# A Fourier layer and a gated convolution on one core: the first batch's feature D/2 through the FFT, five narrowings shared between two engines, and batch 2's folds in earlier steps

## The chip, the cores and the metric

The kernel runs on one core of a Trainium2 chip. A core has five engines that work side by side, each through its own queue in order: TensorE (PE) multiplies matrices, VectorE (DVE) and ScalarE (ACT) work element by element, GpSimd (POOL) does small element work and issues indirect loads, SyncE (SP) issues transfers. ACT and POOL issue some transfers too. Waits between engines are semaphores. The metric is device time in microseconds: the median of three runs. A profile of one further execution shows what each engine did and when.

## The reference

The input x has 8 batches of 3136 rows and 256 columns. Each batch goes through a two-dimensional Fourier transform, of which the real part is kept, and then through a gated feed-forward layer with a three-tap convolution along the rows:

```python
X = np.fft.fft(x, axis=1)
X = np.fft.fft(X, axis=2)
a = X.real.astype(np.float32)

h = np.maximum(a @ w_in, 0.0)                    # 256 -> 1024
hp = pad(h, one row of zeros on each side)
conv_out = sum(conv_w[k] * hp[:, k:k + S, :] for k in range(3))
gate = 1.0 / (1.0 + np.exp(-conv_out))
return (h * gate @ w_out).astype(np.float32)     # 1024 -> 256
```

x is float32. The weights `w_in` (256 x 1024), `conv_w` (3 x 1024) and `w_out` (1024 x 256) arrive as float64, and the kernel makes float32 of them itself: that is a narrowing.

## The kernel before

**The transform.** Rows n and S - n, and columns d and D - d, are folded onto each other, so that the transform over rows becomes a few real products with cosine and sine tables. For each batch VectorE folds the input: `fold_ops(b)` gives 14 operations, seven for each half of x, which end in two tiles `w` of folded features. TensorE multiplies these with the tables (`tabs`, in a version for even and one for odd rows) in units (`units(b)`): matrix products, then a copy by ScalarE (`copy`), then sums by VectorE (`fin`). The results are PT and QT (`PQ[b]`), with 1569 row frequencies each. The transform over columns is merged with `w_in` into a matrix `G` (`blocks(i)`, `column(i)`). The product with PT (`pa`) and the product with QT (`pb`) give by their sum a front row, and by their difference the mirrored back row.

**Feature D/2** (column 128 of x) has only a cosine part, and it does not fit into the 128 partitions of PT beside the other 128. For batches 1 to 7 the class `Feature` computes its transform as a 56 x 56 FFT: a gather of the 3136 single elements, tables made on ScalarE (`tables`), and four stages (`stage`: matrix products, two twiddle products on VectorE, matrix products, a copy and a store to `ed` in DRAM). `spread` reads `ed` back, repeated over all partitions, into `eb`. `seed(s)` writes `eb` times a column `ge` into the bank `pa` before the products of step s add to it. For batch 0 before the change, the odd half of this feature stands in row 127 of QT and the even half in a tile `ea`; a unit `feature` and a row `er` on one partition collect both. The first four steps add it by a one-row product of `er` and `left`; from the fifth step on `seed` is used, and two steps write the whole bank `pa` once beforehand (`start_all`).

**The loop.** A step s is one of 8 batches, 4 chunks of row frequencies and 8 blocks of 128 hidden features: 256 steps, 32 for each batch. A cycle t works on several steps at once, and the loop at the end of the kernel gives the order in every queue: `sigmoid` of step t - 2, `products` and `copies` of step t + 1, `combine` of step t, `seed` of step t + 2, `first_tap` of step t, `other_taps` of step t - 1, `gate` of step t - 2, `mm2` of step t - 3. The first 20 steps (`triple`) let TensorE add the sine product to `pa` once more, so that VectorE combines only the back rows.

**Work beside the steps** is put into cycles by hand with `at(cycle, where, fn)`, and `where` says at which place of a cycle it runs. The list `ends` holds for each batch the cycle in which its folds end and its units start; the folds of batch b run from `ends[b - 1]` to `ends[b]`, its units from `ends[b]` to three cycles before its first step. `free` moves a fold to a later cycle where one is `taken`. The loads of batch b + 1 follow the folds of batch b at a fixed distance.

**The start.** SyncE loads the first half of x of batch 0; GpSimd issues four indirect loads of mirrored rows, writes one element that lets SyncE load the second half (`held`), issues four more, and writes one element that lets the tables load. VectorE folds. TensorE meanwhile multiplies folded data into an unused bank (`keep_on`), so that it is busy before the first real product. The order behind it is: narrow the first quarter of `w_in`, mirror the tables on ScalarE, four odd units, narrow the second quarter, the even units, `blocks(0)`, narrow the third quarter, and the steps. The fourth quarter is narrowed in cycle 0, `w_out` in cycles 2, 3, 5 and 7.

**A narrowing** is seven VectorE operations on 512 elements of each partition: three make the exponent, one puts the sign in, two make the mantissa, and one multiplies them.

Of the kernel before, what the change touches and what calls it, by code (L numbers as in the profile page):

```python
# [30 lines left out]
FIRST = 4  # L31
# [7 lines left out]
def kernel(  # L39
# [33 lines left out]
    ep = ctx.enter_context(tc.tile_pool(name="ep", bufs=2))  # L73
    erp = ctx.enter_context(tc.tile_pool(name="erp", bufs=1))
# [28 lines left out]
    xh, wt, ea = {}, {}, {}  # L103
# [3 lines left out]
    sg = const.tile([P, 2, 2], F32, name="sg")  # L107
    nc.gpsimd.memset(sg[:, 0], -1.0)
    nc.gpsimd.memset(sg[:, 1], 1.0)
# [33 lines left out]
    def fold_ops(b):  # L143
# [3 lines left out]

        def half(h):
# [27 lines left out]
            def feats(odd):  # L176
                def f():
                    if h == 0 and odd:
                        wt[b] = [wp.tile([P, 4, HQ, P], F32, name="w", tag="w%d" % i) for i in range(2)]
                        if b == 0:  # L180
                            ea[b] = ep.tile([P, 2, HQ], F32, name="ea", tag="ea")
                            nc.gpsimd.memset(wt[b][0][0:KR, 2:4, :, P - 1:P], 0.0)
# [6 lines left out]
                    if b:  # L189
                        nc.gpsimd.memset(wt[b][odd][k, 2:4, qs, P - 1:P], 0.0)  # L190
                    elif odd:
                        gt(w[k, 2:4, qs, P - 1], t()[k, 7:5:-1, :, P], sg[k], op=ALU.mult)
                    else:
                        nc.gpsimd.tensor_copy(ea[b][k, :, qs], v[:, :, :, P])
# [10 lines left out]
    PQ, eb, er = {}, {}, {}  # L205
# [36 lines left out]
    class Unit:  # L242

        def __init__(self, b, mms, copy, fin, own=False):
            self.own, self.b, self.mms, self.copy_, self.fin_ = own, b, mms, copy, fin

        def matmuls(self, i, n):
            if i == 0:
                self.p = spare() if self.b == 0 and not self.own else psd.tile([P, 512], F32, name="pd", tag="pd")
# [22 lines left out]
    def units(b):  # L272
# [54 lines left out]
        def feature():  # L327

            mms = []
            for i in range(2):  # L330
                for j, qs in enumerate(((3, 1), (2, 0))):
                    for c in range(2):
                        n = HO // 2 + 1 - c
                        o = 32 * (2 * j + c)
                        mms.append(product((slice(o, o + 1), slice(0, n)),
                                           lambda k, q, c=c: ea[b][0:k, c, q:q + 1], 0, qs[i],
                                           slice(c, HE, 2), i == 0, i == 1))

            def copy(p):
                a_["e"] = [asp.tile([P, HO + 2], F32, name="as", tag="as") for _ in range(2)]  # L340
                for j in range(2):
                    for c in range(2):
                        n = HO // 2 + 1 - c
                        o = 32 * (2 * j + c)
                        nc.scalar.copy(out=a_["e"][c][0:1, j * n:(j + 1) * n], in_=p[o:o + 1, 0:n])

            def fin(p):
                t = er[b]
                nh = HO // 2
                for c in range(2):  # L350
                    n = nh + 1 - c
                    a, bb = a_["e"][c][0:1, 0:n], a_["e"][c][0:1, n:2 * n]
                    gt(t[:, 2 * c:Q4 + 1:4], a, bb, op=ALU.add)
                    gt(t[:, M - 2 * c:Q4:-4], a[:, 0:nh], bb[:, 0:nh], op=ALU.subtract)
            return Unit(b, mms, copy, fin, True)

# [3 lines left out]
        def row():  # L360
            er[b] = erp.tile([1, NK], F32, name="er", tag="er")
            nc.sync.dma_start(out=er[b], in_=PQ[b][1][P - 1:P, :])
# [257 lines left out]
    def start_all(p, l, r):  # L620

        mm(p, l, r, True, True)
# [333 lines left out]
```

## Time and profile before

| what | us |
|---|---|
| runs | 1223.03, 1222.69, 1222.80 |
| median | 1222.8 |
| the profiled execution, and its span | 1223.94, 1222.2 |
| first element operation of the folds | 8.38 |
| tables in place, mirroring starts | 22.95 |
| first product of the first unit | 25.77 |
| first product of step 0 | 44.3 |
| first product of step 1 (cycle 0 starts) | 47.4 |
| start of cycle 36 | 234.8 |
| start of cycle 125 | 642.8 |

The span runs from the first to the last instruction of the program in the profile; the profiled execution's own time lies 1.7 us above it. The profile names engines PE, DVE, ACT, POOL and SP as above, and PEld for the loading of weights into TensorE. A row of the timeline has a start, a duration, engine, line of the kernel, operation and tiles, out<-in; the brackets give idle time of the engine before it, and what ended that. All matrix products stand under line 94, so they are told apart by their tiles: `pb` and `pa` are the products of a step, `po` the output products of a step (and, at the start, spare banks), `pd` the products of the units and of the FFT.

### The profile page before, as it was taken

Reading aid. Unit: us, or ns where it says so; the run is one execution under the profiler, and the core shown is the slowest. Engines: PE = TensorE matmul, PEld = TensorE weight load, DVE = VectorE, ACT = ScalarE, POOL = GpSimd, SP = SyncE. Lnnn points to the kernel's source line nnn. Section 1 sums busy time; section 2 is a strip of 40 time slices with the busy share of each in tenths; the row PEclk is TensorE's granted clock in tenths of the full one; section 3 lists DMA queues with packets and bytes.
Section 4 is the critical chain, followed back from the end, with each engine's and each line's share of the span. In section 5 each row is a group of like instructions: output and inputs, shape, how many; then the busy total and the mean of one; then the engine's idle time right before and its main releaser. Section 6 shows DMA issues by size and latency. Waiting matters only on the chain.

```text
span 1222.2 us, 15450 instructions
## 1 busy us (share of the span) xinstructions
PE 1187.9 (97%) x4876; PEld 907.5 (74%) x4876; DVE 1126.0 (92%) x1696; ACT 877.0 (72%) x1832; POOL 370.9 (30%) x474
## 2 busy tenths in 40 slices
PE   5999999999999999999999999999999999999998
PEld 4676777667777777677777777777777787777776
DVE  7799978998999999999999999999998888899996
ACT  2467666777677777777777777777777777788884
POOL 5224532244142413242324242232222122222222
PEclk9999999999999999999999999999999999999999
DMA  9512242112031210211111020310001000110000
GB/s 235 180 8 79 81 48 60 54 54 72 6 99 42 75 50 32 76 55 53 53 57 59 22 79 27 86 47 26 27 1 53 31 26 27 46 33 27 26 27 31
DMA packets 70213, 66.30 MB, mean 54 GB/s; under 512 B 28123, under 2 KB 57827, under 8 KB 70131
## 3 DMA queue, kind: packets, MB, share of 16 engines
q1 hardware_dynamic: 64493, 52.18, 15.0%
q0 software_dynamic: 5120, 12.85, 3.4%
q8 instruction: 39, 0.64, 0.2%
q14 instruction: 43, 0.35, 0.1%
q10 hardware_dynamic: 518, 0.28, 0.1%
HBM read 39.53 MB, written 25.74 MB: 53 GB/s over the span
## 4 chain that ended last, share of the span: by engine, by line
PE 68%; DVE 22%; issue 4%; ACT 2%; DMA 0%; DVEq 0%; SPq 0%; ACTq 0%
PE po L94 42%; PE pb L94 10%; PE pa L94 10%; DVE g L698 7%; PE pd L94 7%; DVE h L686 4%; DVE g L719 3%; DVE xh L158 2%; DVE xh L169 1%; ACT nb L675 1%; DVE w L186 1%; DVE w L187 1%; DVE xh L173 0%; ACT g L711 0%; DVE pt L291 0%
## 5 line engine op out<-in xcount | busy, mean ns | idle before, releaser
L94 PE MATMUL po<-wout,g 128*128 128x256 f32 x3072 | 709.9, 381 | 13.8 <-DVE g L719 13.3
L94 PEld LDWEIGHTS po<-wout,g 128*128 128x128 f32 x3072 | 579.0, 190 | 168.8 <-DVE g L719 50.7
L698 DVE SCALAR_TENSOR_TENSOR g<-h,cw,g 128x770 f32<-128x770 f32 (+1 forms) x512 | 548.9, 1072 | 9.3 <-ACT g L692 0.2
L718 POOL TENSOR_TENSOR g<-g,h 128x385 f32<-128x385 f32 (+1 forms) x256 | 232.5, 909 | 781.3 <-ACT g L711 523.1
L711 ACT ACTIVATE g<-g 128x385 f32<-128x385 f32 (+2 forms) x512 | 244.4, 527 | 196.8 <-DVE g L698 196.2
L675 ACT ACTIVATE nb<-pb 128x386 f32<-128x386 f32 (+2 forms) x472 | 208.1, 494 | 85.9 <-PE pb L94 85.2
L686 DVE CUSTOM_DVE_ANT_0 h<-pa,nb 128x386 f32<-128x386 f32 (+2 forms) x492 | 255.6, 559 | 3.7 <-ACT h L672 3.7
L692 ACT ACTIVATE g<-h,cw 128x770 f32<-128x770 f32 (+1 forms) x256 | 243.4, 951 | 0.2 <-DVE h L686 0.2
L94 PE MATMUL pb<-qt,G 127*128 127x387 f32 (+2 forms) x512 | 212.8, 496 | 0.0
L94 PE MATMUL pa<-pt,G 128*128 128x387 f32 (+2 forms) x512 | 211.9, 495 | 0.0
L641 ACT ACTIVATE pa<-eb,ge 128x387 f32<-128x387 f32 (+2 forms) x252 | 151.7, 602 | 1.3 <-PE pa L94 0.7
L94 PEld LDWEIGHTS pa<-pt,G 128*128 128x128 f32 x512 | 96.9, 189 | 73.5 <-issue 17.9
L719 DVE TENSOR_TENSOR g<-g,h 128x385 f32<-128x385 f32 (+1 forms) x256 | 146.2, 571 | 0.9 <-ACT g L711 0.9
L94 PE MATMUL pd<-tab,w 98*128 98x196 f32 (+3 forms) x448 | 122.5, 374 | 0.0
L133 POOL DMA_INDIRECT xh<-in_x_dram,idx x64 | 106.5, 1665 | 13.4 <-issue 9.6
L94 PEld LDWEIGHTS pb<-qt,G 127*128 127x128 f32 x512 | 94.6, 190 | 17.4 <-issue 0.9
L94 PEld LDWEIGHTS pd<-tab,w 98*128 98x128 f32 (+1 forms) x448 | 84.0, 191 | 12.5
L738 ACT COPY os<-po 128x256 f32<-128x256 f32 x196 | 57.6, 394 | 8.4 <-PE po L94 4.6
L158 DVE TENSOR_TENSOR xh<-xh 98x1020 f32<-98x1020 f32 (+1 forms) x32 | 40.8, 1283 | 2.4 <-DMA xh<-in_x_dram,idx 2.4
L169 DVE TENSOR_TENSOR xh<-xh 98x1024 f32<-98x1024 f32 (+1 forms) x32 | 42.1, 1314 | 0.1
L291 DVE TENSOR_TENSOR qt<-as,pd 128x197 f32<-128x197 f32 (+1 forms) x14 | 7.2, 516 | 21.7 <-ACT as L287 21.7
L291 DVE TENSOR_TENSOR pt<-as,pd 128x197 f32<-128x197 f32 (+1 forms) x14 | 7.3, 520 | 20.2 <-ACT as L287 20.2
(114 smaller groups left out, 405.6 us busy)
## 6 DMA issues: line engine op xcount, KB each, us to landing
out_dram<-os SPq DMA_DIRECT2D x192, 128.0 KB
xh<-in_x_dram SPq DMA_DIRECT2D x16, 784.0 KB
eb<-ed SPq DMA_DIRECT2D x16, 193.5 KB
tab<-dft_seq_dram SPq DMA_DIRECT2D x4, 589.5 KB
raw<-in_moe_w_in_dram SPq DMA_DIRECT2D x4, 512.0 KB
raw<-in_moe_w_out_dram SPq DMA_DIRECT2D x1, 2048.0 KB
eb<-ed SPq DMA_DIRECT2D x8, 209.0 KB
eb<-ed SPq DMA_DIRECT2D x8, 193.0 KB
```

The source lines that it names most:

```text
L94: nc.tensor.matmul(o, l, r, start=start, stop=stop, skip_group_check=True)
L133: nc.gpsimd.indirect_dma_start(out=xh[b, h][0:NP, 7 - m].rearrange("p q d -> p (q d)"), out_offset=None, in_=bass.AP(tensor=x.tensor, offs ...
L158: vt(a[:, :, :, 1:D], a[:, :, :, 1:D], r[:, :, :, D - 1:0:-1], op=ALU.add)
L641: act(pa[s][:, 0:n], eb[b, c], AF.Copy, scale=ge[:, f:f + 1])
L675: act(nb[s][:, i, cols], p[:, cols], AF.Copy, scale=-1.0 if i else 1.0)
L686: nc.vector._custom_dve(TENSOR_ADD_SAT, out=to, in0=a[:, cols], in1=c[:, i, cols], s0=BIG, s1=0.0)
L692: act(gs[s], hs[s][:, 0:n], AF.Copy, scale=cw[:, 0, s[2]:s[2] + 1])
L698: stt(out=g, in0=h[:, k:k + n], scalar=cw[:, k, f:f + 1], in1=g, op0=ALU.mult, op1=ALU.add)
L711: act(gs[s][:, c], gs[s][:, c], AF.Sigmoid)
L718: gt(g[:, p], g[:, p], h[:, p], op=ALU.mult)
L719: vt(g[:, v], g[:, v], h[:, v], op=ALU.mult)
L738: nc.scalar.copy(out=osb[:, j % 2], in_=pt[:, j % 2])
```

## The change

The change does three things, with what follows from them.

Batch 0's feature D/2 goes through the same FFT as the other batches'. The gather is issued by ScalarE right behind the load of the convolution weights, then come the table rows (`load`, which was a part of `place`). ScalarE makes the FFT's tables before it mirrors the others; the four stages stand between the sixth and the seventh of the first half's folds; GpSimd issues the first `spread`. The row `er`, the unit `feature`, the one-row products, the copies to `left` and `start_all` go. Every step gets a seed, so `column(0)` comes before `blocks(0)` and `column(1)` before the loop. Eight filler products of 512 columns take the place of sixteen of 256; two of them write both banks of `pa`.

In five narrowings (the fourth quarter of `w_in` and all of `w_out`) ScalarE makes the exponent by one Relu in place of two VectorE operations, `left` serves as room for the mantissa, and the sign comes in later.

The folds of batch 2 run in cycles 20 to 35, those of batch 3 from 36 to 60, those of batch 4 from 61 to 92; the units of batches 2, 3 and 4 start at 36, 61 and 93. The last operations of batch 1's units no longer keep folds out of their cycles.

```diff
     def feats(odd):
...
-        if b:
-            nc.gpsimd.memset(wt[b][odd][k, 2:4, qs, P - 1:P], 0.0)
-        elif odd:
-            gt(w[k, 2:4, qs, P - 1], t()[k, 7:5:-1, :, P], sg[k], op=ALU.mult)
-        else:
-            nc.gpsimd.tensor_copy(ea[b][k, :, qs], v[:, :, :, P])
+        nc.gpsimd.memset(w[k, 2:4, qs, P - 1:P], 0.0)
...
+        def load(self):
+            n = (RC + NQ - 1) // NQ
+            for r, v in enumerate(self.l):
+                for s in range(2):
                     w = v.shape[2]
                     nc.scalar.dma_start(out=v[1:1 + n * NQ, s], in_=bass.AP(
...
-        def gather(self, b, b0):
-            nc.sync.dma_start(out=self.y[self.K, b - b0].unsqueeze(2), in_=bass.AP(
+        def gather(self, b, b0, eng):
+            eng.dma_start(out=self.y[self.K, b - b0].unsqueeze(2), in_=bass.AP(
...
-    def narrow(dst, raw):
+    low = const.tile([P, 1], F32, name="low")
+    nc.gpsimd.memset(low, -896.0 * 2 ** 23)
+    def narrow(dst, raw, room):
...
         ts(out=d, in0=hi, scalar1=20, scalar2=0x7FF, op0=lsr, op1=ALU.bitwise_and)
-        ts(out=d, in0=d, scalar1=-896, scalar2=0, op0=ALU.add, op1=ALU.max)
-        ts(out=d, in0=d, scalar1=23, scalar2=None, op0=lsl)
-        stt(out=d, in0=hi, scalar=-0x80000000, in1=d, op0=ALU.bitwise_and, op1=ALU.bitwise_or)
-        ts(out=hi, in0=hi, scalar1=0xFFFFF, scalar2=0x100000, op0=ALU.bitwise_and, op1=ALU.bitwise_or)
-        stt(out=lof, in0=lo.bitcast(U32), scalar=2.0 ** -32, in1=hi, op0=ALU.mult, op1=ALU.add)
+        if room is not None:
+            act(d, d, AF.Relu, scale=2.0 ** 23, bias=low[0:d.shape[0]])
+        else:
+            ts(out=d, in0=d, scalar1=-896, scalar2=0, op0=ALU.add, op1=ALU.max)
+            ts(out=d, in0=d, scalar1=23, scalar2=None, op0=lsl)
+            stt(out=d, in0=hi, scalar=-0x80000000, in1=d, op0=ALU.bitwise_and, op1=ALU.bitwise_or)
+        sg = hi
+        if room is not None:
+            c, n = hi.shape[1:]
+            sg = room[:, 0:c * n].rearrange("p (c n) -> p c n", c=c)
+        ts(out=sg, in0=hi, scalar1=0xFFFFF, scalar2=0x100000, op0=ALU.bitwise_and, op1=ALU.bitwise_or)
+        stt(out=lof, in0=lo.bitcast(U32), scalar=2.0 ** -32, in1=sg, op0=ALU.mult, op1=ALU.add)
+        if room is not None:
+            stt(out=d, in0=hi, scalar=-0x80000000, in1=d, op0=ALU.bitwise_and, op1=ALU.bitwise_or)
         stt(out=dst, in0=lof, scalar=2.0 ** -20, in1=dst, op0=ALU.mult, op1=ALU.mult)
...
+    feat = Feature()
     w_cv.load(nc.scalar)
+    feat.place()
+    feat.gather(0, 0, nc.scalar)
+    feat.load()
     for h in range(2):
         for f in load_ops(0, h, nc.sync, nc.scalar, h == 1):
             f()
...
         act(pa[s][:, 0:n], eb[b, c], AF.Copy, scale=ge[:, f:f + 1])
...
-        mm(pa[s][:, 0:n], G[:, 0, fs], PQ[b][0][:, ch.k0:ch.k1], first(s), not triple(s))
-        if first(s):
-            mm(pa[s][:, 0:n], left[0:1, f, :], er[b][:, ch.k0:ch.k1], False, False)
+        mm(pa[s][:, 0:n], G[:, 0, fs], PQ[b][0][:, ch.k0:ch.k1], False, not triple(s))
...
-    def keep_on(n):
-        for _ in range(n):
-            mm(idle[:, 0:2 * P], wt[0][1][0:NP, 1, 0], wt[0][1][0:NP, 0, 0:2], True, True)
+    def keep_on(banks):
+        for p in banks:
+            mm(p.rearrange("p (s q d) -> p s q d", s=2, q=2), wt[0][1][0:NP, 1, 0], wt[0][1][0:NP, 0:2, 0:2],
+               True, True)
...
-    nc.gpsimd.memset(PQ[0][1][96:P, :], 0.0)
-    for f in fold_ops(0):
+    for i in range(3):
+        feat.tables(i)
...
+    ops = fold_ops(0)
+    for f in ops[0:6]:
         f()
+    for i in range(4):
+        feat.stage(i, 0, 1)
+    for f in ops[6:]:
+        f()
+    spread(0, [0], nc.gpsimd)
...
-    keep_on(16)
+    keep_on([idle] * 6)
+    keep_on([psa.tile([P, 512], F32, name="pa", tag="pa") for _ in range(2)])
...
-    flip()
-    store()
-    spread(0, range(len(chunks)))
+    spread(0, range(1, len(chunks)))
     for f in load_ops(1, 0, nc.sync):
         f()
+    column(0)
     blocks(0)
...
-    at(0, "dve", lambda: w_in[3].narrow(0, 2))
-    for i in (0, 1):
-        at(i, "pe", lambda i=i: column(i))
+    room = left.rearrange("p f i -> p (f i)").bitcast(I32)
+    at(0, "dve", lambda: w_in[3].narrow(0, 2, room))
     for cycle, c in ((2, 0), (3, 2), (5, 4), (7, 6)):
-        at(cycle, "dve", lambda c=c: w_out.narrow(c, c + 2))
+        at(cycle, "dve", lambda c=c: w_out.narrow(c, c + 2, room))
...
-    ends = [9] + [max(26 * b - 6, per * (b - 1) - 3) for b in range(1, B)]
+    ends = [9, 20, per + 4] + [per * (b - 1) - 3 for b in range(3, B)]
...
-            taken.add(cs[i + 1])
+            if b > 1:
+                taken.add(cs[i + 1])
...
     copies(steps[0])
+    column(1)
```

## The prediction

> **What bounds the kernel now.** I read the page first, then busy times by stretch, then waits and timeline at the start and around one narrowing.
>
> ```profile
> PE 1187.9 (97%) x4876; PEld 907.5 (74%) x4876; DVE 1126.0 (92%) x1696; ACT 877.0 (72%) x1832; POOL 370.9 (30%) x474
> PE 68%; DVE 22%; issue 4%; ACT 2%; DMA 0%; DVEq 0%; SPq 0%; ACTq 0%
> ```
>
> Both PE and DVE are nearly full, and the chain of what ended last changes between them: the answer differs by stretch. A cycle t of the loop starts with the pb product of step t+1. From those starts I cut the run: cycles 0-8 are 47.4 to 97.1, 9-19 to 151.8, 20-35 to 234.8, 36-60 to 352.2, 61-92 to 497.9, 93-124 to 642.8, 125-156 to 785.7. Columns: stretch, length, then busy us of PE, PEld, DVE, ACT, POOL, clock, DMA share, GB/s.
>
> ```profile
> 0.00:44.30 44.30, 28.62 (x127) 22.21 (x127) 33.94 (x62) 12.38 (x27) 22.09 (x38) 1.00 0.83 235
> 47.40:97.10 49.70, 48.24 (x198) 33.47 (x197) 44.82 (x67) 30.33 (x61) 8.59 (x18) 1.00 0.30 56
> 97.10:151.80 54.70, 52.76 (x211) 37.82 (x210) 54.28 (x68) 39.55 (x99) 29.52 (x27) 1.00 0.24 74
> 151.80:234.80 83.00, 80.79 (x338) 61.01 (x338) 72.62 (x118) 55.38 (x116) 20.04 (x29) 1.00 0.26 50
> 234.80:352.20 117.40, 114.58 (x470) 87.43 (x469) 111.06 (x168) 84.29 (x175) 41.13 (x45) 1.00 0.20 60
> 352.20:497.90 145.70, 144.06 (x590) 110.10 (x589) 138.26 (x212) 107.05 (x223) 49.02 (x61) 1.00 0.18 57
> 497.90:642.80 144.90, 142.38 (x581) 108.27 (x580) 138.10 (x212) 107.37 (x223) 46.63 (x58) 1.00 0.17 55
> 642.80:785.70 142.90, 142.61 (x591) 110.61 (x590) 134.84 (x208) 108.18 (x224) 45.31 (x56) 1.00 0.16 50
> ```
>
> PE's own work needs no busy column: near the end six 256-column matmuls (twelve passes) take 2.59 us and a whole cycle 3.89, so a column costs 1.69 ns. Summed over each stretch's matmuls that gives 46.7, 51.1, 78.7, 112.2, 141.4, 139.7 and 141.4 us for the seven stretches from 47.4 on. The lengths exceed it by 3.0, 3.7, 4.3, 5.2, 4.3, 5.2 and 1.5. The last has 32 cycles with folds and DFT spread over all of them, and nearly no loss; the four before alternate cycles in which DVE has a fold and PE nothing extra (4.6 us against 3.9) with cycles in which PE has DFT matmuls (5.2). Batch 2 is the clearest: folds in 20-45, DFT in 46-60.
>
> The start, first the waits, then the timeline:
>
> ```profile
> ACT tab L239 <- DMA tab<-dft_seq_dram: 16.0, 1, 16.0
> PE pb L94 <- POOL w L188: 8.7, 1, 8.7
> DVE xh L158 <- DMA xh<-in_x_dram,idx: 2.4, 1, 2.4
> ```
>
> ```profile
> 2.01 1.19 POOL L133 DMA_INDIRECT xh<-in_x_dram,idx  x1 [0.26 <-issue]
> 12.98 0.09 POOL L575 MEMSET tab<- 1x1 f32 x1
> 13.10 1.40 SPq L219 DMA_DIRECT2D tab<-dft_seq_dram  x2
> 15.36 5.06 PE L94 MATMUL pb<-w 98*128 98x256 f32 x11 [8.66 <-POOL w L188]
> 19.79 6.14 PE L94 MATMUL pb<-w 98*128 98x256 f32 x22
> ```
>
> POOL issues eight mirrored loads in order; its memsets behind the fourth and the eighth release SP's next loads, so POOL paces all input. PE's fillers run until 25.9, when the DFT starts.
>
> One narrowing (cycle 2):
>
> ```profile
> 57.89 0.56 DVE L686 CUSTOM_DVE_ANT_0 h<-pa,nb 128x385 f32<-128x385 f32 x1 [2.82 <-ACT h L672]
> 58.36 0.42 DVE L515 TENSOR_SCALAR wout<-raw 128x512 int32<-128x512 int32 x1
> 63.86 0.49 ACT L672 ACTIVATE h<-pa 128x385 f32<-128x385 f32 x1 [0.37 <-PE pa L94]
> ```
>
> The ACT row is step 3's relu, behind which the new exponent operation will stand; here it comes 5 us after DVE has its exponent bits.
>
> **What the Trainium skill says.** "ScalarE: Activation LUTs", What ACT_TABLE_LOAD costs: an ACTIVATE with a per-partition pointer takes about 280 ns + 0.833 ns an element; 921 for 770 elements, and the trace has 938: agrees. "TensorE: Matmul & The Clock Gate", What's actually happening: full clock only after a busy window of about 3.4 us that is not aligned to the kernel. The eleven slow filler passes (0.46 us, then 0.28) agree in kind. "DMA: Bandwidth & Descriptors", Queues, rings and completion order: an engine takes turns between its queues packet by packet; no row here shows a gather beside full loads. "GPSIMD Engine Reference", Specifications: POOL shares SBUF interfaces with DVE. Agrees: the two-tap operation takes 1.51 us at 63.31 beside POOL's gate, usually 1.04.
>
> **The change part by part.**
>
> *Front.* POOL gets two iotas, a sign operation that waits for DVE, and four memsets before its first load: 0.2 + 0.16 + 0.19 + 0.90 (their rows at 78-84 us) + about 0.25 of handing over = 1.7 us, and with it the held half of x and the tables. DVE's second fold needs the fourth load (landed 9.39, issue now ends 8.75): I put 1.5 on DVE. The two twiddle products, 112 elements, by the 336-element row (488 ns) less 224 elements[...], are 0.25 each: DVE +2.0 behind them. The gather (three in 64.6-71.1, 0.63 to 0.78 of the DMA engines: 1.75 us of all of them each) and the table rows (0.76) must fit before 10 us, where the share leaves 2.4 us idle; I take 0 beyond the 1.7. Fillers now stand behind the second FFT stage: evens end 15.9 + 1.5, products 0.5, matmuls about 0.9: start 18.8 instead of 15.36. The columns are equal (16 x 256, 8 x 512). At the old 10.5 us they end 29.3, at full clock (6.9) 25.7, when the tables (22.9 + 1.7, then 1.97 of mirroring) bind at 26.6. Bounds for the start of the DFT: +0.8 to +3.6; I take +2.5. Twenty table operations on ACT (4.7 us) lie in its 16 us wait; ACT's issues (1.9 + 4 x 0.77) push the zero rows to 8.6, needed at 17.1: 0. POOL's eb load waits for the feature's store (about 22) and fits POOL's 12.1 us of idleness before 38.37; batch 1's mirrored loads behind it start at 41.6. SP loses two row transfers and one eb load: 0.
>
> *To the first combine.* Out go the feature's matmuls (0.88) and one copy row (0.86), in comes the column (0.97). But DVE's third narrowing, 43.2 to 47.3, is what combine(0) then waits for: 47.35 instead of 48.14, so -0.8.
>
> *Cycles 0-8.* PE loses four one-row products (0.65), the other copy row (0.86) and two 512-column starts (0.86 each), with what lies ahead: 46.7 to 40.3. DVE loses two operations of 0.46 in each of five narrowings: 46.7 to 42.1 by rows. DVE becomes the bound. The exponent costs ACT an estimated 706 ns (first page); DVE covers 1.2 us with the two mantissa operations. Laying the rows of each engine in queue order, DVE waits 0.9 in cycle 0, 3.0 in cycle 2 (step 3's products stand behind blocks, and ACT behind a table load), 0 in cycle 3, 0.5 in 5 and 7: 5.0, against 2.8 now. So 42.1 + 5.0 = 47.1 instead of 49.5: -2.4. Four added seeds (0.59) lie in ACT's idle 1.9 us before each relu; uncovered they cost 0.59 each. The work moved out of cycles 5-13 (ACT, POOL) was hidden: 0, at most -1.
>
> *Cycles 9-19*: DVE-bound by folds that stay: 0.
>
> *Cycles 20-124.* DFT sums stay; folds move. DVE by rows (3.40 a cycle, 3.7 in a last chunk, 1.2 a fold, 0.55 to 0.94 a finish): 20-35 rises 72.8 to 81.3 against PE's 78.7; 36-60 falls to 109.0 against 112.2; 61-92 to 134.6 (141.4); 93-124 to 134.6 (139.7). In 20-28 both have 47 to 49, in 29-35 DVE 33.9 against 29.7: 49.0 + 1.5 + 33.9 = 84.4, +1.5. The others get a loss like that of 125-156, more for 36-60, which inherits DVE's backlog: 114.0, 143.0, 142.0: -3.4, -2.7, -3.0. Together -7.6; bounds -11 and 0. The folds' companions move with them: batch 3's plain load and three zero rows pass output stores on SP, its eight mirrored loads (1.67 us each) and batch 2's feature copies pass gates on POOL. POOL is busy for a quarter to a third of these stretches, and a gate's half is needed a cycle later by PE: 0; a gate that did wait behind a mirrored load would cost PE up to 1 us, eight times. SP never waits long here: 0. Stages of the other batches' FFT stay at 14-18 and 31-35.
>
> *Rest* unchanged in order: 0.
>
> Sum: +2.5 - 0.8 - 2.4 + 0 - 7.6 = -8.3. The profiled execution took 1223.94 (span 1222.2), 1.1 above the median of 1222.8; on the median: **1214.5**.
>
> **Rivals.**
>
> R1, the exponent waits stay as the trace has them. Exponent bits are ready at 49.04, 58.78, 66.09, 76.92, 88.29; the relus ahead end at 51.09, 64.35, 69.78, 79.72, 88.94. Adding 0.7 and taking off 1.2 of cover: 1.6, 5.1, 3.2, 2.3, 0.2 = 12.4 instead of 5.0: 1222. Against: PE is lighter, so the relus come sooner.
>
> R2, spreading gains nothing, because DVE is the bound in 20-60 and its sum (459.5 us in 20-124) is the same: +7.6, 1222. Against: 125-156, where the same sums lose 1.5.
>
> R3, slower: the gather lands late. DVE, ACT and PE all stand in order behind it, before folds, mirroring and fillers. The engines are full (0.99, 1.05) from 10 to 32 us; 3,136 small packets taking turns with 2 KB ones would last until then. Products at 33 instead of 17.4 cost 15.6: 1230. It decides from a landing after 17.4 us, and the gain is gone at 26. Against: idle shares before 10 us and a held second half.
>
> R4, fewer waits in 0-8 and bound -11: 1208.
>
> **How the numbers follow.** Forecast 0.58, R1 0.14, R2 0.10, R3 0.13, R4 0.05. The forecast's own range, from the front's bounds and those of cycles 20-124, is 1209 to 1220. I give 1207 to 1225, which leaves out R3 and a thin low edge. Within 0.2% (2.4 us) is what one cannot tell from no change: most of R1, R2 and the forecast's upper edge, 0.19. Faster 0.66, slower 0.15.
>
> **What would show it.** First mirrored load at 3.7, fillers from about 19, DFT from 28, first product near 46.5; the twiddle products without a wait before them. Five DVE waits on the exponent operation, the longest in cycle 2, 5 us together; four more seeds. 36-124 at about 399 us instead of 408, 20-35 a little longer. A DVE wait for the gather, or a filler start past 22, makes it R3; waits of 12 us, R1.

## The result, and the profile after

The changed kernel took 1223.4 us (median of 4 runs, 1223.07 to 1226.01) beside 1222.8 for the kernel before on the same chip: ratio 1.0009, 95% interval 0.9992 to 1.0027. No change can be told. Forecast was 1214.5. The profiled execution took 1223.58, with a span of 1221.8.

The page of the changed kernel, busy times and the engines' shares of the chain:

```profile
PE 1180.9 (97%) x4834; PEld 902.0 (74%) x4834; DVE 1120.5 (92%) x1688; ACT 880.8 (72%) x1835; POOL 366.7 (30%) x468
PE 72%; DVE 19%; issue 4%; ACT 3%; DMA 2%; POOL 0%; DVEq 0%; SPq 0%; ACTq 0%; POOLq 0%
```

TensorE and VectorE lost 7.0 and 5.5 us of work, and the span hardly moved. In the chain, the share of DMA rises from 0 to 2%. Busy times of the changed kernel, cut at the same cycles as before (columns: stretch, length, busy us of PE, PEld, DVE, ACT, POOL, clock, DMA share, GB/s):

```profile
0.00:52.10 52.10, 29.62 (x109) 19.29 (x109) 35.28 (x66) 13.56 (x45) 19.78 (x44) 1.00 0.97 242
54.90:101.60 46.70, 41.52 (x168) 29.95 (x168) 39.46 (x56) 32.55 (x65) 6.40 (x11) 1.00 0.15 20
101.60:156.40 54.80, 52.83 (x211) 37.80 (x210) 54.38 (x68) 36.80 (x79) 29.53 (x27) 1.00 0.25 74
156.40:241.50 85.10, 82.31 (x338) 61.94 (x338) 80.72 (x129) 55.13 (x116) 29.44 (x37) 0.98 0.31 67
241.50:357.20 115.70, 114.54 (x469) 87.04 (x468) 110.17 (x166) 83.94 (x175) 39.30 (x44) 1.00 0.20 60
357.20:500.10 142.90, 142.60 (x590) 110.40 (x589) 135.01 (x208) 108.55 (x224) 46.01 (x56) 1.00 0.16 50
500.10:642.50 142.40, 141.44 (x582) 108.78 (x582) 134.65 (x209) 108.47 (x224) 45.49 (x57) 1.00 0.16 53
```

| stretch | before | after | difference | forecast |
|---|---|---|---|---|
| to the first product of step 0 | 44.3 | 52.1 | +7.8 | +2.2 |
| from there to cycle 0 | 3.1 | 2.8 | -0.3 | -0.5 |
| cycles 0-8 | 49.7 | 46.7 | -3.0 | -2.4 |
| 9-19 | 54.7 | 54.8 | +0.1 | 0 |
| 20-35 | 83.0 | 85.1 | +2.1 | +1.5 |
| 36-60 | 117.4 | 115.7 | -1.7 | -3.4 |
| 61-92 | 145.7 | 142.9 | -2.8 | -2.7 |
| 93-124 | 144.9 | 142.4 | -2.5 | -3.0 |

(The forecast's first product near 46.5 is +2.2; its +2.5 and -0.8 make +1.7 for the first two rows together.) Behind the first product the loop gained 8.1 us, and the front lost 7.8. The DMA share of the front rose from 0.83 to 0.97.

Two rows of the front before, and then the timeline of the changed front:

```profile
8.38 2.35 DVE L158 TENSOR_TENSOR xh<-xh 98x1020 f32<-98x1020 f32 x2 [2.40 <-DMA xh<-in_x_dram,idx]
22.95 1.97 ACT L239 ACTIVATE tab<-tab 99x392 f32<-99x392 f32 x4 [16.03 <-DMA tab<-dft_seq_dram]
```

```profile
13.90 1.22 DVE L151 TENSOR_TENSOR xh<-xh 98x1020 f32<-98x1020 f32 x1 [2.15 <-DMA xh<-in_x_dram,idx]
20.17 0.44 DVE L397 TENSOR_TENSOR ft<-pd,ft 56x112 f32<-56x112 f32 x2
20.67 0.95 PE L91 MATMUL pd<-ft 56*29 56x56 f32 x8 [4.63 <-DVE ft L397]
21.54 8.71 PE L91 MATMUL pb<-w 98*128 98x512 f32 x12
31.81 2.14 PE L91 MATMUL po<-tab,w 98*128 98x196 f32 x8
35.02 6.22 PE L91 MATMUL po<-tab,w 98*128 98x196 f32 x24 [1.06 <-ACT tab L224]
21.65 0.20 ACT L406 COPY ft<-pd 29x56 f32<-29x56 f32 x1 [3.24 <-PE pd L91]
32.65 0.24 ACTq L408 DMA_DIRECT2D ed<-ft  x1
33.06 1.90 ACT L224 ACTIVATE tab<-tab 99x392 f32<-99x392 f32 x4 [11.21 <-DMA ed<-ft]
```

Three things are to be read from it. VectorE's second fold waits 2.15 us for a mirrored load and starts at 13.90; before, the two stood together from 8.38. The twiddle products stand behind six folds, the second FFT product behind them, and the fillers behind that: they start at 21.54 instead of 15.36. ScalarE has the FFT's result at 21.85 and issues its store at 32.65; the mirroring, which is next in its queue, starts at 33.06 instead of 22.95, and TensorE pauses 1.06 us for it in its first DFT. What held the store is in the chain of waits of the same kernel (start, duration, what):

```profile
8.56 13.18 DMA xh<-in_x_dram
21.75 0.02 issue
21.76 10.81 DMA tab<-dft_seq_dram
32.57 0.02 issue
32.59 0.02 ACTq L408
32.65 0.43 DMA ed<-ft
33.07 1.90 ACT tab L224 x4
```

In the compiled program the transfers of SP and ScalarE take turns over eight semaphores (the records of the trace name them), and each waits until the transfer eight places ahead of it has landed. The gather and the four table rows move every later transfer by five places. So the first load of the other table waited for the second half of x (21.75), and ScalarE's store of 6 KB for that table (32.57).

The DMA engines in the first 20 us, in 40 slices of 0.5 us: share in tenths, GB/s, and the queue that carries ScalarE's transfers (packets, MB, share of 16 engines). First the kernel before:

```profile
DMA  0005349999997785957789999998998999998998
GB/s 0 0 0 70 57 160 336 356 291 291 303 303 176 213 250 172 291 98 201 270 336 369 315 287 217 262 205 197 250 211 220 297 306 226 264 277 239 340 222 202
q10 hardware_dynamic: 61, 0.04, 0.8%
```

Then the changed kernel:

```profile
DMA  0006647999999997897998899999999989999999
GB/s 0 0 0 70 35 115 213 350 348 299 191 60 7 40 177 107 189 262 194 275 208 212 248 232 262 299 229 250 222 221 203 235 197 226 239 240 220 272 218 220
q10 hardware_dynamic: 3463, 0.24, 17.9%
```

Between 5.5 and 7 us the engines are busy for 0.9 of the time or more and move 60, 7 and 40 GB/s, where they moved 303, 176 and 213: the gather's 4-byte packets have their turn. ScalarE's queue takes 17.1% of sixteen engines more, 3.4 us of all of them. About half of that went into slices before 10 us that had been idle (their mean share rises from 0.67 to 0.83). The second fold is 4.4 us late. In a later run without the small packets it is 1.7 us late, about the 1.4 by which GpSimd's first load is issued later (3.43 instead of 2.01); the other 2.7 are the small packets' part.

### The profile page after: what moved, and what is told of

Same layout as the page of the kernel before. It is cut to its first block, busy times and chain, and to the rows that moved or that the text cites. A ratio compares the mean times of both kernels' runs of the same rounds, so it can differ in the third digit from the quotient of the medians.

```text
span 1221.8 us, 15368 instructions
## 1 busy us (share of the span) xinstructions
PE 1180.9 (97%) x4834; PEld 902.0 (74%) x4834; DVE 1120.5 (92%) x1688; ACT 880.8 (72%) x1835; POOL 366.7 (30%) x468
## 3 DMA queue, kind: packets, MB, share of 16 engines
HBM read 39.54 MB, written 25.74 MB: 53 GB/s over the span
## 4 chain that ended last, share of the span: by engine, by line
PE 72%; DVE 19%; issue 4%; ACT 3%; DMA 2%; POOL 0%; DVEq 0%; SPq 0%; ACTq 0%; POOLq 0%
PE po L91 45%; PE pb L91 11%; PE pa L91 10%; DVE g L643 6%; PE pd L91 6%; DVE h L631 3%; DVE g L664 3%; DVE xh L151 2%; ACT nb L620 1%; DMA xh<-in_x_dram 1%; DMA tab<-dft_seq_dram 1%; DVE xh L162 1%; DVE w L176 1%; DVE w L177 1%; ACT g L656 0%
## 5 line engine op out<-in xcount | busy, mean ns | idle before, releaser
L91 PE MATMUL pd<-tab,w 98*128 98x196 f32 (+3 forms) x448 | 126.7, 374 | 0.0
L178 POOL COPY w<-xh 98x4 f32<-98x4 f32 (+1 forms) x32 | 20.4, 639 | 33.1 <-DVE xh L162 17.5
```

The lines of the kernel that those rows point to most:

```text
L91: nc.tensor.matmul(o, l, r, start=start, stop=stop, skip_group_check=True)
```

## The experiments

Each run is compared with the kernel before on its own chip; the first product is that of step 0 in its profile. A profile shows where the time of one execution goes, the medians what an edit is worth.

### The loop's edits without the front

```diff
 # kernel before, plus
-    ends = [9] + [max(26 * b - 6, per * (b - 1) - 3) for b in range(1, B)]
+    ends = [9, 20, per + 4] + [per * (b - 1) - 3 for b in range(3, B)]
-            taken.add(cs[i + 1])
+            if b > 1:
+                taken.add(cs[i + 1])
 # e1_old_front also: narrow(dst, raw, room), with
+    room = left[:, NF // 2:NF].rearrange("p f i -> p (f i)").bitcast(I32)
```

> The kernel before with the loop's two edits only: the new placing of folds and finishes, and the exponents of five narrowings on ScalarE (their spare tile is the other half of `left`, which is free in the first cycles). Batch 0's feature stays the old way, and so does the whole front. Theory A, the loop's gain is real and the front alone lost it: first product at 44.3 as before, cycles 9 to 124 shorter by about 5 us, cycles 0 to 8 by about 1.5 (their other gain came from the dropped one-row products): 1216.3 us, faster by 0.5%. Rival B, the loop's gain in the changed kernel only made up for work that the late front had already let run ahead (loads, DVE), and is gone with an early front: 1221 or more.

> The kernel before with the new placing of folds and finishes alone. Theory A, alternating cycles cost what the sums say: cycles 20 to 124 shorter by about 5 us, cycles 20 to 35 longer by 2, cycles 36 to 124 shorter by 7: 1217.8 us. Rival B, DVE's sum decides and where its folds stand does not matter: 1222.8, no change.

Measured: 1218.45 (ratio 0.9961, 0.9947 to 0.9974) and 1218.79 (0.9963, 0.9949 to 0.9976). In both, cycles 20-35 take 85.0, 36-60 115.7, 61-92 142.9 and 93-124 142.3: as in the changed kernel to 0.1 us. The spreading is worth its 4.9 us with an early front too. The exponents on ScalarE add nothing: cycles 0-8 take 49.7 without them and 50.5 with them. In that part the first run's expectation failed.

### The exponents back on VectorE

```diff
 # changed kernel
-    room = left.rearrange("p f i -> p (f i)").bitcast(I32)
+    room = None
```

> The changed kernel with the five narrowings wholly on DVE again (seven operations, none on ScalarE), all else as changed. Theory A, DVE bounds cycles 0 to 8 and the offload is what shortened them: ten operations of 0.43 to 0.46 come back, the 5.8 us of waits for the exponent do not all go: cycles 0 to 8 at 48.5 to 49.5 instead of 46.7, 1225.5 us. Theory B, the waits for ScalarE (5.8 us) already cost what the offload took off DVE (4.5), and the shorter cycles come from TensorE's dropped one-row products, copy rows and starts: 46.7 give or take 0.6, no change against the changed kernel.

Measured: 1224.38 (1.0010, 1.0004 to 1.0017); cycles 0-8 took 46.8, although TensorE's clock was at half for 3.4 us of that. Theory B. Busy times of this run in cycles 0-8:

```profile
54.50:101.30 46.80, 42.70 (x168) 31.18 (x169) 44.84 (x66) 29.54 (x60) 6.62 (x11) 0.96 0.16 20
```

VectorE works 44.84 us here and 39.46 in the changed kernel, for the same length. The waits of VectorE in those cycles of the changed kernel say where the 5.4 us went:

```profile
DVE wout L480 <- ACT wout L468: 4.3, 3, 3.8
DVE h L631 <- ACT h L617: 1.6, 2, 0.8
DVE win L480 <- ACT win L468: 1.5, 1, 1.5
```

Five exponent operations hand back 5.8 us of waiting. So cycles 0-8 are shorter because TensorE lost its one-row products, rows and starts, not because VectorE lost operations; the last version below, with VectorE's operations as before, bears it out.

### The front: packets and places

```diff
 # e3_contiguous, changed kernel (batch 0 only)
-ap=[[RC * D, RC], [D, RC], [1, 1]]
+ap=[[RC, RC], [1, RC], [1, 1]]
 # e4_store_pool, changed kernel (batch 0 only)
-nc.scalar.dma_start(out=ed[b0:b1]...
+nc.gpsimd.dma_start(out=ed[b0:b1]...
```

> The changed kernel with batch 0's gather replaced by a read of 56 whole runs of 56 elements from the same rows' memory: 56 packets instead of 3,136, the same place in ScalarE's queue, everything else alike. Batch 0's feature is then not the reference's. Theory A, the small packets themselves push the loads of x back: the second fold at about 11.7 us instead of 13.9, the fillers at about 19.3 instead of 21.5, the first product near 49.7 instead of 52.1: 1221 us, 2.4 less than the changed kernel. Rival B, the order of issues and waits behind earlier transfers (table rows, zero rows) does it: less than 0.5 us between the two.

Measured: 1219.58 (0.9974, 0.9964 to 0.9983). Fillers start at 18.85, first product at 47.9: 4.2 us earlier, more than the 2.4 expected. Theory A. The mirroring also comes earlier (28.91), since the loads that hold the store land earlier. With the packets went some of ScalarE's time for issuing (last section), so the gain is that of both.

> The changed kernel with the store of batch 0's feature issued by POOL instead of ScalarE. In the changed kernel this store stands on ScalarE until the first load of the other table has landed (32.6 us), and the mirroring stands behind it. Theory A, that hold is what makes TensorE wait 1.7 and 1.1 us in its first DFT: mirroring starts at about 25, when its own table has landed, the two waits go, first product near 49.4: 1220.7 us. Rival B, the mirrored table itself lands only at about 33: mirroring starts there all the same, no change. Rival C, TensorE waits for something else next (the old fillers end at 31.8): part of the 2.7 only.

Measured: 1222.40 (0.9991, 0.9983 to 1.0000), at most 2 us less than the changed kernel. The mirroring starts at 28.87, so its own table lands there and not at 25. The expectation had added a wait of TensorE and one of its weight load that are the same pause: 1.06 us, not 2.7. It is gone, and the first product still comes at 52.2. VectorE now waits 1.4 us for the second quarter of `w_in` (landed 43.2), which keeps TensorE's first column back, and in this profile the clock fell behind it, which cost 0.4 us more (2.43 instead of 1.99 us for the eight products of a block of `G`). Rival C. GpSimd had started batch 1's mirrored loads at 32.1 instead of 40.9; a later run comes back to that.

```diff
 # e6_added_gather and e7_added_run, kernel before, behind w_cv.load
+    more = const.tile([P, RC], F32, name="more")
+    nc.scalar.dma_start(out=more[0:RC].unsqueeze(2), in_=bass.AP(tensor=x.tensor, offset=x.offset + P,
+        ap=[[RC * D, RC], [D, RC], [1, 1]]))      # e7: [[RC, RC], [1, RC], [1, 1]]
```

> The kernel before with one gather added, nothing else: the same 3,136 elements of batch 0's middle column, issued by ScalarE right behind the first load, into a spare tile that nobody reads. Theory A, the DMA engines are the bound of the start and the small packets take their time from the loads of x: 2.5 us, first product at 46.8 instead of 44.3, 1225.3 us. Rival B, they fit into the DMA engines' idle time before 10 us, as the prediction had it: at most 0.5 us.

> The same with 56 whole runs of 56 elements instead of the gather: one transfer more in the order of issues, 56 packets. Theory A: no change (1222.8, within 0.6). Rival C, one transfer more in the order shifts every later load to a wait behind another earlier load, and that alone costs: 1 us or more.

Measured: 1224.71 (1.0013, 1.0006 to 1.0019) with the gather and 1223.56 (1.0001, 0.9993 to 1.0010) with the run: one transfer more in the order costs nothing that can be told. The timeline of the kernel with the added gather:

```profile
10.33 1.22 DVE L158 TENSOR_TENSOR xh<-xh 98x1020 f32<-98x1020 f32 x1 [3.92 <-DMA xh<-in_x_dram,idx]
15.86 9.96 PE L94 MATMUL pb<-w 98*128 98x256 f32 x32 [8.71 <-POOL w L188]
25.74 2.22 PE L94 MATMUL po<-tab,w 98*128 98x196 f32 x8
26.15 1.97 ACT L239 ACTIVATE tab<-tab 99x392 f32<-99x392 f32 x4 [16.51 <-DMA tab<-dft_seq_dram]
```

The first fold is 1.95 us late and the mirroring 3.2, as theory A says, yet the DFT starts at 25.74 (25.77 before) and the first product is 0.5 us late, as rival B says. The fillers hide it: they need only the first odd features and cover TensorE until 25.7. The medians say 1.6 us (0.7 to 2.3), between the two theories (the profile of the kernel before is itself 1.1 us above its median), so how much is hidden stays open. The gather's price in the DMA engines follows from its queue's share in the first 20 us of this run:

```profile
q10 hardware_dynamic: 3211, 0.05, 11.3%
```

(11.3% - 0.8%) of 16 engines for 20 us are 33.6 us of engine time for 3,150 packets more: 10.7 ns each. That is 2.1 us of all sixteen. Recorded times of packets can overlap (the share reaches 1.48 from 6.5 to 7 us), but the bytes agree: 4.00 MB in these 20 us for 4.54 before, at 262 GB/s (10 to 20 us before) 2.1 us less.

```diff
 # e9_fillers_first, changed kernel: ops[0:4]; stage 0; fillers; ops[4:6]; stage 1; other folds
+    feat.stage(0, 0, 1)
+    keep_on([idle] * 6)
+    keep_on([psa.tile([P, 512], F32, name="pa", tag="pa") for _ in range(2)])
...
     mirror_tables(2)
+    for i in (2, 3):
+        feat.stage(i, 0, 1)
+    spread(0, [0], nc.gpsimd)
 # e14_fillers_held, kernel before, keep_on
-            mm(idle[:, 0:2 * P], wt[0][1][0:NP, 1, 0], wt[0][1][0:NP, 0, 0:2], True, True)
+            mm(idle[:, 0:2 * P], wt[0][0][0:NP, 1, 0], wt[0][0][0:NP, 0, 0:2], True, True)
```

> The changed kernel, only the order on TensorE, ScalarE and DVE in the front: the eight filler matmuls and the mirroring stand ahead of the second FFT product, the copy and the store of its result, not behind them; the gather and the table rows load as in the changed kernel. Theory A, the fillers' place behind the second FFT product is the larger part of the loss (21.5 us instead of 15.4): fillers start at 17.5 to 18, the DFT when DVE has the second half's odd features, about 27.3, the mirroring when its table lands, 25 to 29, TensorE waits at most 2 us for it, first product at 48.5 to 49.5 instead of 52.1: 1220.5 us, 3 less than the changed kernel. Rival B, the loads decide, not the order: the third filler row or the DFT waits, first product at 51 or later, less than 1.2 us gained. Rival C, as in the run with the store on POOL: DFT early, but the second narrowing waits for its weights until 43 and TensorE idles ahead of the first column: 1222.

Measured: 1220.18 (0.9968, 0.9955 to 0.9981), with gather and table rows as in the changed kernel. Its timeline:

```profile
17.79 8.84 PE L91 MATMUL pb<-w 98*128 98x512 f32 x12 [0.43 <-POOL w L179]
28.28 0.58 PE L91 MATMUL pd<-ft 56*29 56x56 f32 x8
28.79 8.21 PE L91 MATMUL po<-tab,w 98*128 98x196 f32 x32
47.68 0.92 PE L91 MATMUL pb<-qt,G 127*128 127x386 f32 x2 [0.46 <-ACT G L557]
```

Fillers 3.75 us earlier, the DFT 3.0, no wait inside it, first product 4.4 us earlier. Theory A.

> The run with the fillers first, and batch 0's gather replaced by the read of 56 whole runs (the feature of batch 0 is then not the reference's): both suspected causes taken away at once. Theory A, order and packets are two separate losses (4.4 and 4.2 us of the 7.8): first product at 44 to 45, 1216.5 us, what the prediction had summed up. Theory B, they are one loss seen twice (small packets delay the second FFT product, and the fillers stand behind it): each run has already taken most of it, first product at 46.5 or later, 1218.5 us or more.

Measured: 1215.91 (0.9938, 0.9922 to 0.9955), what theory A expected. Against the kernel before, the four ratios are +0.09% for the changed kernel, -0.26% without the small packets, -0.32% with the fillers first, -0.62% with both: 4.3 and 5.0 us alone, 8.7 together. The intervals make each of these uncertain by 2 to 3 us, but both together gain clearly on either alone (-0.62% against -0.26% and -0.32%): two losses, which nearly add. The profile of this run has the DFT at 24.96 but the first product only at 46.4; the reason is the clock (last section).

> The kernel before, one thing changed: the fillers read the even features instead of the odd ones, so that they start some 4 us later (about 18.5 instead of 15.4), without any gather or FFT. Theory A, a later filler start moves the DFT by as much, because nothing else is late there: DFT at 28 to 29, first product 46.5 to 47.2 instead of 44.3, 1225.5 us. Rival B, the DFT has slack behind the fillers: first product at 45.5 or earlier.

Measured: 1224.92 (1.0014, 1.0007 to 1.0020). Fillers at 18.30, DFT at 28.55, first product at 47.05: 2.9, 2.8 and 2.8 us late. Theory A: without any gather, a later filler start comes through one to one in the trace; the medians show 1.7 us.

### Fronts with the feature later

```diff
 # e8_late_feature, changed kernel: place, table rows behind the other loads
     mirror_tables(0)
+    feat.gather(0, 0, nc.scalar)
     mend_row(1, half)
 # e10: gather as in the changed kernel; table rows by nc.gpsimd behind the mirrored loads; tables()
 # behind the mirroring; stages 0, 1 ahead of the odd units' last quarter, 2, 3 ahead of narrow(1)
-    spread(0, range(1, len(chunks)))
+    spread(0, range(len(chunks)))
 # e11: e10 with
+    spread(0, [0], nc.gpsimd)
+    spread(0, range(1, len(chunks)))
```

> The changed kernel with batch 0's feature moved back: no sign or table work ahead of POOL's mirrored loads, table rows loaded behind the zero rows, the gather issued by ScalarE only after the first mirroring (near 26 us), the two FFT products inside the DFT's second half, all four loads of its result on SP. Same arithmetic. Theory A, what the front lost is the DMA time and the POOL and DVE time ahead of the loads: fillers start at 15.4 again, DFT at 25.7, first product near 44.0, cycles 0 to 8 at 46.7 as in the changed kernel: 1215.5 us, less than both and less than the kernel with the spreading alone (1218.8). Rival B, the gather is late or slow beside the full loads: TensorE waits for its first product or the first steps for their loaded result, 2 to 5 us: 1218 to 1221. Rival C, table rows ahead of the tables in the order of issues hold SP's loads: DFT starts 1 to 3 us late.

Measured: 1235.6 (1.0104, 1.0089 to 1.0119), rival B and worse. TensorE's waits from 20 to 66 us:

```profile
PE pd L91 <- DMA ft<-in_x_dram: 8.5, 1, 8.5
PE po L91 <- issue: 5.6, 1, 5.6
```

ScalarE's gather was held until 32.85 by the transfer eight places ahead, with the mirroring behind it (5.6), and then took 16.7 us to land beside the loads of `w_in` and `w_out`. The forecast's R3 had that mechanism; it needs the gather among full loads, and in the changed kernel it stands ahead of them. Behind the long waits the clock was at half for 20 us (31.9 to 38.7 and 45.5 to 59.2), which is part of the loss.

> The changed kernel with the front's parts put apart: the gather as the second transfer on ScalarE as in the changed kernel, but the table rows loaded by POOL behind the eight mirrored loads, sign and zero work of POOL behind its first two copies, the table operations on ScalarE behind the mirroring, the first FFT product ahead of the last quarter of the DFT's first half, the second behind it, all loads of the result on SP. Same arithmetic. From the run with one added gather (first product +0.5) and the page of the kernel with the spreading alone (44.1): TensorE loses the old feature's matmuls and copy row (1.74) and gets column and two FFT products (2.8): first product 45.5, cycles 0 to 8 at 46.7: 1217.0 us, less than both kernels and 1.8 less than the spreading alone. Rival B, the table rows beside full loads land late, as the late gather did (16.7 us), and ScalarE holds the mirrored copies: 1219 to 1223. Rival C, the result's store and loads are late for the first seed (needed near 45.5): TensorE waits ahead of its second product, 1219.

Measured: 1224.62 (1.0007, 0.9999 to 1.0015), first product at 52.6; none of the three. Some 1.5 us of the 52.6 are the clock's, which fell here too (3.53 instead of 1.99 us for the eight products of a block). VectorE's waits from 20 to 52 us in this run:

```profile
DVE win L470 <- DMA raw<-in_moe_w_in_dram: 5.1, 2, 3.9
```

Nothing held GpSimd any more, so batch 1's mirrored loads ran from 29.8, beside `w_in`. The next run puts GpSimd's wait back:

> The run with the gather first and the FFT late, one thing changed: the first load of the feature's result is issued by POOL again, so that batch 1's four mirrored loads stand behind it in POOL's queue (near 41 us) instead of starting at 29.8. Theory A, those four loads running beside w_in's second quarter are what made DVE wait 3.9 us for it and TensorE 3.9 us ahead of the first column: the wait goes, the first product comes at 48 to 49 instead of 52.6: 1220.5 us. Rival B, w_in's second quarter is late for the earlier gather and tables alone: wait of 3 us or more stays, 1223 or more.

Measured: 1224.37 (1.0014, 1.0007 to 1.0020). In its profile VectorE's wait for `w_in` is gone and the first product comes at 47.8, theory A; then ScalarE waits 2.0 us for the feature's loaded result and TensorE 1.65. But this profiled execution (1221.14) is the fastest of its twenty, and the medians of the two runs don't differ. Its clock was 0.999 on average and that of the other nineteen 0.993 to 0.997, so a falling clock may have eaten the gain; no run separates that. That the mirrored loads made `w_in` late is shown; a gain in time is not.

### A version that beats both

```diff
 # kernel with the spreading alone
-FIRST = 4
+FIRST = 2
-                start_all(pa[s].rearrange("p (t n) -> p t n", t=2), dm[:, 0, 0], w4[0])
-    keep_on(16)
+    keep_on([idle] * 6)
+    keep_on([psa.tile([P, 512], F32, name="pa", tag="pa") for _ in range(2)])
     copies(steps[0])
+    column(1)
```

> The kernel with the spreading alone and the old way of batch 0's feature, with three things taken over from the changed kernel's idea: only the first two steps (not four) get the feature by a one-row product, steps 2 and 3 take it as a seed; the last fillers are 512 columns wide and fill the two accumulator banks, so that the two 512-column starts at steps 4 and 5 go; column(1) is computed ahead of the loop. Same arithmetic. Theory A, TensorE bounds cycles 0 to 8 in the kernel with the spreading alone, and the work taken away (two row products 1.3, two starts 1.7, one row of a block 0.4) shortens them until DVE's 46.7 binds: cycles 0 to 8 at 47.0 to 48, first product at 44.5 to 45 (the column moves ahead of the loop): 1216.5 us, less than both kernels, without a gather. Rival B, seed(2) waits for the feature's load (issued at 44.6, needed at 48.4), or DVE waits: no gain over the spreading alone, 1218.5 or more.

Measured: 1217.73 (0.9955, 0.9942 to 0.9969), 5.5 us less than before and the least of all runs that compute the whole. Theory A; cycles 0-8 take 47.7, from 48.0 on:

```profile
48.00:95.70 47.70, 43.15 (x178) 31.08 (x179) 44.79 (x67) 29.54 (x61) 8.20 (x18) 1.00 0.33 56
```

TensorE's busy time there fell from 48.24 to 43.15, and VectorE's 44.8 is now the larger. Its lead over the spreading alone is 1.3 us at cycle 253 in the profiles; the intervals of the two overlap.

## Why the prediction was wrong

**The front, the step that failed.** It put +2.5 on the start of the DFT, with bounds +0.8 to +3.6; it came 6.0 late, and the first product 7.8 late instead of 2.2 (1.1 more by the pause for the mirroring, 0.7 by the DFT's length and the pauses around the first column). Three of its terms were wrong; the 1.5 us for GpSimd's work ahead of its loads was about right (1.7 without the small packets).

- "The gather ... and the table rows ... must fit before 10 us, where the share leaves 2.4 us idle; I take 0 beyond the 1.7." They took 3.4 us of all engines, not the 2.5 that it put (1.75 and 0.76), and the idle slices were not free: the engines idled there because GpSimd had yet to issue its next loads, and these then came behind the small packets. Taking the small packets out gave back 4.3 us.
- "Fillers now stand behind the second FFT stage: ... start 18.8": 21.54, with all that the folds ahead were late. Putting them first gave back 5.0 us (this includes the next point). The added gather alone shows why the place mattered: in the old order 2 to 3 us of late loads cost 0.5 in the trace and 1.6 in the medians, because the fillers covered a part of them. The edit took the cover away and sent the late loads at the same time.
- The store was taken to follow the result, "about 22", and the mirroring to start when its table lands. The store waited until 32.6 for a transfer eight places ahead, and the mirroring behind it: a pause of 1.1 us in TensorE's first DFT. The forecast counted the queues past which each transfer moved, not the semaphores that they share.

**Cycles 0-8: a near number from a wrong reason.** -2.4 forecast, -3.0 measured. The exponents' waits were well sized (5.8 against 5.0), but the forecast took VectorE as the bound that the offload relieves. Without the offload the cycles are as long; TensorE's dropped work is the cause.

**Cycles 20-124: the mechanism right, the size off.** -4.9 instead of -7.6. 20-35 (+2.1 for +1.5), 61-92 and 93-124 (-2.8 and -2.5 for -2.7 and -3.0) are near. The term that was off is 36-60, -1.7 for -3.4: a loss of 3.5 over TensorE's 112.2 us where 1.8 was put. The backlog of VectorE from 20-35 that it named is at most part of this: cycles 36-40 take 23.7 us for 22.2 of TensorE's columns, and the other 2.0 us are spread over 41-60. Where they come from was not tried. The spreading alone confirms the whole: 0.9963.

**The rivals and the range.** R2 (spreading gains nothing) fell, as did R1 (the time was near its 1222, but the exponents are not the cause). That 1223.4 lies within the stated 1207 to 1225 is luck: a gain and a loss of 8 us met there, and no rival had both. The upper end of "the forecast's own range" was too low by its own terms: the bounds of +3.6 for the front and 0 for 20-124 add to 1223.2, not 1220. R3 saw the danger at the right place with another course: the gather landed early and pushed everything else back. Its sign, a filler start past 22, was missed by half a microsecond.

## What to carry to other kernels

A stretch with idle transfer engines is no room if the next loads are only waiting for their issuer: price a new transfer against the loads that come right after it, and by packets, not by bytes. Filler work that covers late loads is part of the critical path's safety; when a change moves it behind something, count the lateness that it used to hide. Before a transfer is added ahead of others, follow which earlier transfer each later one will wait for. And look at the clock before explaining a late product: in four of these profiles it fell ahead of the loop.

## What the runs showed of the hardware

A 4-byte packet took 10.7 ns of an engine by its records. Over all sixteen engines that is 2.1 us for the gather; beside full loads it took 16.7 us to land. "DMA: Bandwidth & Descriptors", Queues, rings and completion order, has the engines take turns between queues by packets, which agrees in kind.

Issuing the gather took ScalarE 1.00 us and the four table rows behind it 6.47; behind the 56 whole runs the same four took 3.39.

The clock fell without a long pause. In the run with both causes taken away, around its first product (columns as above):

```profile
40.00:42.00 2.00, 1.49 (x12) 1.19 (x10) 2.00 (x7) 0.32 (x1) 1.48 (x2) 1.00 1.07 251
42.00:44.00 2.00, 1.75 (x5) 1.33 (x5) 1.93 (x7) 0.16 (x1) 1.59 (x2) 0.64 0.70 200
44.00:46.00 2.00, 1.92 (x5) 1.01 (x3) 1.90 (x4) 0.41 (x2) 1.29 (x5) 0.51 0.70 260
46.00:48.00 2.00, 1.62 (x5) 1.01 (x6) 0.85 (x2) 1.83 (x4) 0.00 (x0) 1.00 1.07 265
```

The granted clock falls to 0.51, and eight 256-column products take 3.59 us instead of 1.99. TensorE had paused 0.51 and 0.25 us around eight one-column products, no more. "TensorE: Matmul & The Clock Gate", What's actually happening, asks for an idle window of about 3.4 us; even with the one-column products counted as idle, TensorE idled here for 1.8 us.

What tips it can be estimated from the traces. In all sixteen the clock changes only in steps of 3.41 us, so the time behind the first rise can be cut into windows of that length. Twelve passes of 256 columns take 2.59 us, so a column of a pass counts 0.845 ns, and a window's columns give the share of it in which columns streamed. Each of the eleven falls from full clock ahead of the kernel's end follows a window with a share of 0.41 or less. No window above 0.41 was followed by one, and of those below two were not (0.37 and 0.40). In the run above the share was 0.41; with the fillers first it was 0.51, and the clock stayed. So it fell behind windows that were thinly filled, not only behind idle ones. No run varied this share on purpose.

The changed kernel has one such fall, in cycles 20-35:

```profile
212.50:215.90 3.40, 1.46 (x7) 1.08 (x7) 3.36 (x7) 1.70 (x5) 0.86 (x1) 1.00 0.18 48
215.90:219.40 3.50, 3.50 (x10) 2.60 (x9) 3.46 (x4) 1.83 (x4) 3.19 (x3) 0.51 0.00 0
```

There it cost nothing that can be told: VectorE was busy nearly throughout, and these cycles take 85.0 us with the spreading alone as well, where the clock stayed full. In the run with both causes taken away the loss, 1.6 us in the profile, is why the first product came at 46.4 and not under 45; two other executions of that kernel, at clocks of 0.999 and 1.000, took 1215.39 and 1215.88 us, this one 1217.57.
